# Handing out a side tile's twelve products in pieces of four between the units of windowed attention

## The chip, the cores and the metric

The kernel runs on one core of a Trainium2 chip. The metric is the device time of one execution, in microseconds (us); the median of several runs is compared. One execution of each kernel is also taken with the hardware profiler, and everything said about where time goes comes from that execution's trace. The engines are called as the profile calls them: PE does the matrix products (PEld is its weight load), ACT the activations, DVE and POOL element-wise work, and SP issues the DMAs.

## The reference

Four transformer layers without a feed-forward part, alternately of two kinds, on a sequence of S = 2048 rows of width D = 512, with 32 heads of 16. Kind A is causal attention within a sliding window of 256; kind B is full attention. Each layer adds its output to its input.

```python
def _A_ref(x, wqkv, wo):                     # B the same, without the mask
    B, S, D = x.shape
    H = 32; Dh = D // H; W = 256
    qkv = (x @ wqkv).reshape(B, S, 3, H, Dh).transpose(2, 0, 3, 1, 4)
    q, k, v = qkv[0], qkv[1], qkv[2]
    scores = jnp.einsum("bhqd,bhkd->bhqk", q, k) * (Dh ** -0.5)
    idx = jnp.arange(S)
    mask = (idx[:, None] - idx[None, :] >= 0) & (idx[:, None] - idx[None, :] < W)
    scores = jnp.where(mask[None, None], scores, -1e9)
    p = _softmax(scores, axis=-1)
    o = jnp.einsum("bhqk,bhkd->bhqd", p, v)
    return o.transpose(0, 2, 1, 3).reshape(B, S, D) @ wo

x = A_x
x = x + _A_ref(_layernorm(x), A_wqkv, A_wo)
x = x + _B_ref(_layernorm(x), B_wqkv, B_wo)
x = x + _A_ref(_layernorm(x), A_wqkv, A_wo)
x = x + _B_ref(_layernorm(x), B_wqkv, B_wo)
```

## The kernel before, in words

Layers 0 and 2 are the sliding ones, layers 1 and 3 the full ones. Within a layer the queries are taken in four chunks `c` of 512 rows, and the 32 heads in eight groups `qd` of four.

**Units of attention.** In a sliding layer, `attn_win` cuts the work of one (c, qd) into three units `u`, so a layer has 4 x 8 x 3 = 96 units. A unit has three steps. First `exps` runs twice, once for each pair of heads: PE writes scores into a PSUM tile `s` (L731), ACT turns it into probabilities `e` (L735), and POOL zeroes the two triangles of the window's edges in `e` (L802, L805). The pool of `s` has two buffers, and a unit uses both, so the first scores of the next unit wait until ACT has read the first tile, and its second scores until ACT has read the second. Then, two units late (`flush(2)`), PE multiplies the probabilities by the values (the products into `acc`, L812). Then `sd.step()` may put other work on PE.

**Side work.** That other work is everything that is not attention: the projections to keys, queries and values (`project`, `values`) for later chunks and for the next layer, and the output projection (`wo`) with the layer norm behind it. It is cut into tiles: a tile is twelve matmuls, four blocks of the inner dimension times three terms of a split into half-precision parts, accumulated in one PSUM bank and then read out. In a sliding layer the key and query tiles are read out by ACT (`sp`, L506), followed by a square on ACT (`sq`, L519) and a second half on DVE (L509); value tiles by ACT (L637); output tiles by DVE (L653). These tiles come from a pool of two banks, `b`, which they share with the sums of squares (`squares`, L546), taken in rotation. Each work is a Python generator; `mms` is the part that records the matmuls. In a full layer `mms` yields after each of its matmul steps; in a sliding layer it does not yield, so a tile is one run of twelve.

**What sets the order.** PE's instructions keep the order in which the program records them. The other engines' order in a sliding layer is made by a scheduler from readiness and priority. `Side` is the planner: it holds the works of one chunk and their cost on a model clock (0.222 us for a matmul, `MM`). At step k of n, work is due up to cost x k / (n - 2), and `step` goes on taking from the works until what is spent reaches what is due:

```python
            s0, due = self.spent, self.cost * self.k / (self.steps - 2)
            while self.q and self.spent < due and self.spent - s0 < 3:
                c = self.one()
                if c is None or c < 0 and self.spent - s0 >= 2 and due - self.spent < 4:
                    break
```

A negative cost marks the end of a tile. `one` picks the first work that is ready, unless a tile is open (`PH["busy"]`), in which case it must go on with the same work (`PH["last"]`); before, only the full layers open a tile in this sense. `finish` gives out what is left at the end of a chunk, and the parts between the layers (`all_of`) run outside any phase. `phase(l)` sets `PH["full"]` and `PH["win"]`.

Of the kernel before, what the change touches and what calls it, by code (L numbers as in the profile page):

```python
# [30 lines left out]
SCALE = DH ** -0.5  # L31
MM = 0.222
HEAD_START = 100
EB, XB, XNB, WB, VB, OB = 6, 4, 4, 2, 3, 5
RINGS = WB, VB
L_MIN = 2.0 ** -90
# [153 lines left out]
def fast_path(ctx, tc, flag, a_x, a_wqkv, a_wo, b_wqkv, b_wo, out):  # L190
# [199 lines left out]
    def mms(ps, pairs, after=1.6, us=MM):  # L390


        PH["busy"] = PH["full"]
        for i, (a, b) in enumerate(pairs):
            if PH["full"]:
                for g in range(0, P, 32):
                    for r in range(2):
                        k = slice(R * r, R * r + R)
                        nc.tensor.matmul(ps[g:g + 32, r], a[k, g:g + 32], b[k], start=(i == 0), stop=(i == len(pairs) - 1),  # L399
                                         skip_group_check=True)  # L400
            else:
                nc.tensor.matmul(ps, a, b, start=(i == 0), stop=(i == len(pairs) - 1))  # L402
            spent(us)
            if i < len(pairs) - 1:
                if PH["full"]:
                    yield us
            else:
                PH["free"] = clock[0] + (2.0 if PH["full"] else after)
                PH["busy"] = False
    TERMS = ((0, 0), (0, 1), (1, 0))  # L410

    def join(dst, ps, scale=1 / WS):
# [65 lines left out]
    def project(l, s, c, act, ht=None):  # L478


        ty, n = l % 2, f"{l}_{s}_{c}" + ("" if ht is None else f"_h{ht}")
        w = weights(ty, s, n, *((0, D, 0) if ht is None else (ht * P, (ht + 1) * P, not act)))
        yield wait(8)
        xc = XC[l, c]
        if s == 0:
            dst = rows(qs[ty, c])
        elif ty == 0:
            dst = rows(kw[c])
        else:
            dst = rows(kf)[:, :, c * QC:(c + 1) * QC]  # L490
        sqs = {}
        for t in range(NHT) if ht is None else (ht,):
            ps = bank()
            w0 = t * P if ht is None else 0
            yield from mms(ps, [(w[:, k, a, w0:w0 + P], xc[:, b, k, :]) for a, b in TERMS for k in range(NC)], 2.2)
            if not PH["full"]:
                settle(not sqs)
            with tc.high_priority(HEAD_START):
                if PH["full"]:
                    drain(1)  # L500
                    j = vp.tile([P, QC], F32, name=f"j{n}_{t}", tag="j")
                    join(j, (ps[:, 0], ps[:, 1]))
                else:
                    sp = vp.tile([P, 2, QC], F16, name=f"sp{n}_{t}", tag="sp", bufs=3)
                    if act:
                        nc.scalar.activation(sp[:, 0], ps, AF.Copy, scale=1 / WS)  # L506
                    else:
                        nc.vector.tensor_scalar(sp[:, 0], ps, 1 / WS, None, op0=ALU.mult)
                    nc.vector.scalar_tensor_tensor(sp[:, 1], ps, 1 / WS, sp[:, 0], op0=ALU.mult, op1=ALU.subtract)  # L509
            full = PH["full"]  # L510

            def parts(t=t, sp=None if full else sp, j=j if full else None):
                if full:
                    sp = vp.tile([P, 2, QC], F16, name=f"sp{n}_{t}", tag="sp", bufs=3)
                    nc.vector.tensor_copy(sp[:, 0], j)  # L515
                    nc.vector.tensor_tensor(sp[:, 1], j, sp[:, 0], ALU.subtract)
                sq = vp.tile([P, QC], BF16, name=f"sq{n}_{t}", tag="sq", bufs=NHT)
                if act:
                    nc.scalar.activation(sq, sp[:, 0], AF.Square)  # L519
                else:  # L520
                    nc.gpsimd.tensor_tensor(sq, sp[:, 0], sp[:, 0], ALU.mult)  # L521
                sqs[t] = sq

                d = dst[8 * t:8 * t + 8].rearrange("h (d b) n -> (h d) b n", b=4)
                if s:
                    nc.sync.dma_start(d[:, 0:2], sp[:, 0:1].broadcast_to([P, 2, QC]))
                    nc.sync.dma_start(d[:, 2], sp[:, 1])
                else:
                    nc.sync.dma_start(d[:, 0:2], sp)
                    nc.sync.dma_start(d[:, 2], sp[:, 0])  # L530
            soon(0, 1.2, parts)
            yield -MM if PH["full"] else -12 * MM
        return sqs

    def squares(n, sqs):
# [71 lines left out]
    def values(l, c, act, halves=(0, 1), tiles=range(4)):  # L607

        n = f"{l}_{c}_{halves[0]}_{tiles[0]}"
        HH, D0, D1 = H // 2, halves[0] * D // 2, (halves[-1] + 1) * D // 2  # L610
        w = weights(l % 2, 2, f"v{n}", D0, D1)
        yield wait(8)
        xc = XC[l, c]
        dst = {}
        if l % 2:
            for h in halves:
                m = l, h, c // 2
                if m not in V:
                    V[m] = wp.tile([P, 8, HH, DH + 1], F32, name=f"vt{l}_{h}_{c // 2}", tag="vf", bufs=NQ)
                    nc.gpsimd.memset(V[m][:, :, :, DH:], 1.0)  # L620
                dst[h] = V[m][:, 4 * (c % 2):4 * (c % 2) + 4]
        else:
            vt = V[l, c] = wp.tile([P, 4, H, DH + 1], F32, name=f"vt{n}", tag="vw", bufs=VB)
            nc.gpsimd.memset(vt[:, :, :, DH:], 1.0)
        us = MM * (D1 - D0) / D
        for i in tiles:
            ps = bank()[..., :D1 - D0]
            yield from mms(ps, [(xc[:, b, k, i * P:(i + 1) * P], w[:, k, a, :D1 - D0]) for a, b in TERMS for k in range(NC)], us=us)
            src = ps.rearrange("p r (h d) -> p r h d" if PH["full"] else "p (h d) -> p h d", d=DH)
            for x, h in enumerate(halves if l % 2 else (None,)):  # L630
# [9 lines left out]
            yield -us if PH["full"] else -12 * us  # L640

    def wo(l, c, tail):

# [3 lines left out]
        for i in range(4):  # L647
# [11 lines left out]
            yield -MM if PH["full"] else -12 * MM  # L659
        if PH["full"]:  # L660
            yield from norm(l + 1, c, xs, tail)

# [220 lines left out]
    class Side:  # L883
# [13 lines left out]
        def one(self, force=False):  # L897

            drain()
            if PH["full"] and PH["busy"]:  # L900
                return self.piece(PH["last"])
            if force:
                self.prefetch()
# [3 lines left out]
            if now:  # L907
                i = now[0]
# [332 lines left out]
```

## Time and profile before

| | |
|---|---|
| median of 3 runs | 2760.06 us (2759.93 to 2761.41) |
| the profiled execution | 2759.5 us, of which its span is 2757.7 us |
| PE busy | 2496.1 us, 91% of the span |
| ACT busy | 2362.9 us, 86% |
| DVE busy | 1094.9 us, 40% |
| POOL busy | 515.8 us, 19% |
| mean granted TensorE clock | 0.988 |

The shares are averages over stages with different limits. The units of layer 0 lie between about 53 and 435 us of the span, those of layer 2 between about 1448 and 1727 us; the full layers take most of the rest. A row of the wait view names who waited, for whom, the total, the number of waits and the longest; a row of a timeline gives the start, the length and, in brackets, the idle time before it with what ended it.

### The profile page before, as it was taken

What the parts mean: (1) busy time and instruction counts of PE and PEld (TensorE: products, weight loads), DVE (VectorE), ACT (ScalarE), POOL (GpSimd) and SP (SyncE); (2) the same over time, 40 slices, a digit from 0 to 9 for tenths busy, and PEclk for the clock granted to TensorE, in tenths of its full rate; (3) what the DMA queues carried; (4) which work ended last, traced back from release to release, by engine and by line L of the source; (5) the groups of instructions that cost most, each with busy time, mean ns of one, the idle gap of its engine ahead of it and who ended that gap; (6) DMA issues with size and microseconds to landing.
All of it is one profiled execution on the core that took longest, in us unless ns stands there. A gap on an engine that the chain in (4) does not pass through costs nothing.

```text
span 2757.7 us, 112292 instructions
## 1 busy us (share of the span) xinstructions
PE 2496.1 (91%) x50513; PEld 1100.3 (40%) x50513; DVE 1094.9 (40%) x2314; ACT 2362.9 (86%) x2683; POOL 515.8 (19%) x1074
## 2 busy tenths in 40 slices
PE   7888989999989999999998898899899999998987
PEld 3233334444433344444443333534444444433332
DVE  5564554122343335325326566323333333333333
ACT  4556654899999999999995667399999999999997
POOL 1445552001000000100105678100000000000000
PEclk9999999999999999999999999999999999999999
DMA  8888856322342224324225565623232333333332
GB/s 286 226 241 240 244 178 191 96 83 82 100 120 79 86 93 137 102 78 126 93 73 169 157 181 143 175 72 109 84 107 90 98 97 104 112 104 123 114 120 103
DMA packets 335035, 359.67 MB, mean 130 GB/s; under 512 B 113616, under 2 KB 250320, under 8 KB 328144
## 3 DMA queue, kind: packets, MB, share of 16 engines
q1 hardware_dynamic: 334544, 352.40, 42.3%
q8 instruction: 397, 6.50, 1.0%
q14 instruction: 94, 0.77, 0.1%
HBM read 239.60 MB, written 96.99 MB: 122 GB/s over the span
## 4 chain that ended last, share of the span: by engine, by line
ACT 56%; PE 23%; issue 11%; DVE 5%; DMA 3%; POOL 2%; SPq 0%; ACTq 0%; DVEq 0%; POOLq 0%
ACT e L735 55%; PE b L402 10%; PE acc L812 3%; PE acc L779 3%; PE bs L402 2%; PE s L731 2%; PE s L727 2%; PE b L399 1%; POOL e L802 1%; POOL e L805 1%; DMA qt<-qs 1%; DMA kt<-kw 0%; DMA wr<-in_A_wo_dram 0%; DVE ot L694 0%; DMA w<-wd 0%
## 5 line engine op out<-in xcount | busy, mean ns | idle before, releaser
L735 ACT ACTIVATE e<-s 128x1024 f32<-128x1024 f32 (+2 forms) x2432 | 2238.8, 1058 | 121.0 <-PE s L731 95.3
L779 PE MATMUL acc<-e,vt 64*17 64x512 f32 x16384 | 1085.0, 590 | 1.3 <-issue 1.3
L727 PE MATMUL s<-qt,kt 64*32 64x512 f16 x16384 | 849.0, 380 | 130.4 <-ACT e L735 106.6
L727 PEld LDWEIGHTS <-kt 64*32 64x32 f16 x16384 | 406.7, 89 | 944.2 <-issue 868.8
L779 PEld LDWEIGHTS acc<-e,vt 64*17 64x17 f32 x16384 | 280.5, 92 | 61.1 <-issue 1.5
L805 POOL TENSOR_SCALAR_AFFINE_SELECT e<-e 128x256 f32<-128x256 f32 x512 | 224.9, 446 | 196.5 <-ACT e L735 195.4
L802 POOL TENSOR_SCALAR_AFFINE_SELECT e<-e 128x256 f32<-128x256 f32 x448 | 198.1, 449 | 114.1 <-ACT e L735 112.3
L712 POOL TENSOR_TENSOR oh<-o,oh 128x512 f16<-128x512 f32 x31 | 36.1, 1165 | 938.1 <-DVE oh L711 884.8
L812 PE MATMUL acc<-e,vt 128*17 128x384 f32 (+2 forms) x2816 | 204.7, 396 | 5.3 <-POOL e L802 4.0
L731 PE MATMUL s<-qt,kt 64*128 64x384 f16 (+2 forms) x1408 | 129.0, 280 | 64.0 <-ACT e L735 38.2
L415 DVE TENSOR_SCALAR sa<-acc 128x512 f32<-128x512 f32 x64 | 44.3, 692 | 335.4 <-PE acc L779 335.4
L402 PE MATMUL b<-xc,w 128*128 128x512 f16 x696 | 166.1, 390 | 7.0 <-DMA w<-wd 5.8
L677 DVE SCALAR_TENSOR_TENSOR x<-b,x 128x512 f32<-128x512 f32 x122 | 83.9, 688 | 193.0 <-PE b L399 189.8
L402 PEld LDWEIGHTS <-w 128*128 128x128 f16 x816 | 77.4, 100 | 122.8 <-issue 35.8
L521 POOL TENSOR_TENSOR sq<-sp 128x512 bf16<-128x512 f16 x28 | 41.0, 1463 | 442.2 <-DVE sp L515 427.6
L506 ACT ACTIVATE sp<-b 128x512 f16<-128x512 f32 x58 | 34.7, 598 | 103.3 <-PE b L402 91.2
L731 PEld LDWEIGHTS <-kt 64*128 64x128 f16 x1408 | 54.4, 94 | 167.6 <-issue 137.0
L521 POOL TENSOR_TENSOR sq_h<-sp_h 128x512 bf16<-128x512 f16 x27 | 40.1, 1484 | 409.8 <-DVE sp_h L515 409.8
L399 PE MATMUL b<-wo,oh 64*32 64x512 f16 x2592 | 109.9, 376 | 6.2 <-DVE x L677 3.1
L399 PE MATMUL b<-xc,w 64*32 64x512 f16 x2688 | 110.9, 376 | 3.0 <-DVE j L416 2.3
L399 PE MATMUL b<-xc,w_h 64*32 64x512 f16 x2592 | 104.4, 376 | 4.1 <-DVE km L562 3.9
L415 DVE TENSOR_SCALAR j_h<-b 128x512 f32<-128x512 f32 x27 | 18.7, 691 | 218.7 <-PE b L399 187.6
(136 smaller groups left out, 1874.8 us busy)
## 6 DMA issues: line engine op xcount, KB each, us to landing
kt<-kf SPq DMA_DIRECT2D x128, 512.0 KB
qt<-qs SPq DMA_DIRECT2D x128, 256.0 KB
xd<-x SPq DMA_DIRECT2D x96, 256.0 KB
x<-xd SPq DMA_DIRECT2D x96, 256.0 KB
w<-wd SPq DMA_DIRECT2D x22, 1024.0 KB
kt<-kw SPq DMA_DIRECT2D x64, 256.0 KB
qs<-sp SPq DMA_DIRECT2D x48, 256.0 KB
wo<-wd SPq DMA_DIRECT2D x12, 1024.0 KB
```

Of the source, the lines that this page charges most:

```text
L399: nc.tensor.matmul(ps[g:g + 32, r], a[k, g:g + 32], b[k], start=(i == 0), stop=(i == len(pairs) - 1), skip_group_check=True)
L402: nc.tensor.matmul(ps, a, b, start=(i == 0), stop=(i == len(pairs) - 1))
L415: nc.vector.tensor_scalar(dst, ps[0], scale, None, op0=ALU.mult)
L521: nc.gpsimd.tensor_tensor(sq, sp[:, 0], sp[:, 0], ALU.mult)
L677: nc.vector.scalar_tensor_tensor(xs[i], p, 1 / WS, xs[i], op0=ALU.mult, op1=ALU.add)
L727: nc.tensor.matmul(ps[g:g + 32, h], kt[R * h:R * h + R, pr, kc + g:kc + g + 32], qt[R * h:R * h + R, pr], start=True, stop=True, skip_grou ...
L731: nc.tensor.matmul(ps[:, h, s0:s0 + wd_], kt[R * h:R * h + R, pr, kc:kc + P], qt[R * h:R * h + R, pr, qc:qc + wd_], start=True, stop=True)
L735: nc.scalar.activation(e[:, :, w0:w1], ps[:, :, w0:w1], AF.Exp, scale=SCALE)
L779: nc.tensor.matmul(acc[r][32 * h:32 * h + DH + 1, :], V[l, qd // 4, j // 8][k, j % 8, 4 * (qd % 4) + h, :], es_[h // 2][k, h % 2, :], star ...
L802: nc.gpsimd.affine_select(v, v, pattern=[[0, 2], [-1, P]], compare_op=ALU.is_gt, fill=0.0, base=0, channel_multiplier=1)
L805: nc.gpsimd.affine_select(v, v, pattern=[[0, 2], [1, P]], compare_op=ALU.is_ge, fill=0.0, base=0, channel_multiplier=-1)
L812: nc.tensor.matmul(a[32 * h:32 * h + DH + 1, q * P:(q + nb) * P], V[l, (4 * c + j) // 4][:, j % 4, 4 * qd + h, :], es_[h // 2][:, h % 2, s ...
```

## The change

In a sliding layer a tile may now stop after four and after eight of its twelve matmuls. `mms` marks the tile as open in sliding layers too, and yields after each piece of four the cost of four. `last` gives the cost of a tile's last piece, 4 x 0.222 us in a sliding layer where it was 12 x 0.222. An open tile is carried on before any other work is picked. Full layers and the parts between the layers keep their steps.

```diff
+PIECE = 4
...
     def mms(ps, pairs, after=1.6, us=MM):
-        PH["busy"] = PH["full"]
+        PH["busy"] = PH["full"] or PH["win"]
         for i, (a, b) in enumerate(pairs):
...
             spent(us)
             if i < len(pairs) - 1:
                 if PH["full"]:
                     yield us
+                elif PH["win"] and i % PIECE == PIECE - 1:
+                    yield PIECE * us
             else:
                 PH["free"] = clock[0] + (2.0 if PH["full"] else after)
                 PH["busy"] = False
+    def last(us):
+        return -(1 if PH["full"] else PIECE if PH["win"] else 12) * us
...
-            yield -MM if PH["full"] else -12 * MM          # project; wo the same, values with us
+            yield last(MM)
...
         def one(self, force=False):
             drain()
-            if PH["full"] and PH["busy"]:
+            if PH["busy"]:
                 return self.piece(PH["last"])
```

**PE, layer 2, the second chunk, between two units.** `s_1_2_0` and `s_1_2_1` are scores of neighbouring units, `acc` the product with the values of an earlier unit, `b` an output tile's bank. Before:

```order
L731 MATMUL s_1_2_0_1_29868<-qt_1_2_29739,kt_1_2_29738 128x384
L812 MATMUL acc_82<-e_1_1_1_0_29776,vt_0_0_0_15544 17x256 x2
L812 MATMUL acc_82<-e_1_1_1_1_29785,vt_0_0_0_15544 17x256 x2
L812 MATMUL acc_82<-e_1_1_1_0_29776,vt_1_0_0_21586 17x256 x2
L812 MATMUL acc_82<-e_1_1_1_1_29785,vt_1_0_0_21586 17x256 x2
L731 LDWEIGHTS kt_1_2_29738
L731 MATMUL s_1_2_1_0_29886<-qt_1_2_29739,kt_1_2_29738 128x256
```

And now, in the changed kernel:

```order
L819 MATMUL acc_82<-e_1_1_1_1_29774,vt_1_0_0_21586 17x256 x2
L403 LDWEIGHTS oh_0_5_29428
L403 MATMUL b_29806<-wo_0_29669,oh_0_5_29428 128x512
L403 LDWEIGHTS oh_0_7_29666
L403 MATMUL b_29806<-wo_0_29669,oh_0_7_29666 128x512
L403 LDWEIGHTS oh_0_7_29666
L403 MATMUL b_29806<-wo_0_29669,oh_0_7_29666 128x512
L403 LDWEIGHTS oh_0_7_29666
L403 MATMUL b_29806<-wo_0_29669,oh_0_7_29666 128x512
L738 LDWEIGHTS kt_1_2_29723
L738 MATMUL s_1_2_1_0_29886<-qt_1_2_29724,kt_1_2_29723 128x256
```

Where the products with the values were followed at once by the next unit's scores, four of an output tile's twelve matmuls now stand between them.

**ACT, layer 2, around the end of a query tile.** `e_1_0_0` to `e_1_0_2` are the three units of one head group, `sp_0_3_0` and `sq_0_3_0` the reading out and the square of a query tile. Before:

```order
L735 ACTIVATE e_1_0_0_1_29612<-s_1_0_0_1_29607 128x1024
L506 ACTIVATE sp_0_3_0_29634<-b_29621 128x512
L735 ACTIVATE e_1_0_1_0_29646<-s_1_0_1_0_29641 128x1024
L519 ACTIVATE sq_0_3_0_29637<-sp_0_3_0_29634 128x512
L735 ACTIVATE e_1_0_1_1_29655<-s_1_0_1_1_29650 128x1024
```

And now:

```order
L742 ACTIVATE e_1_0_0_1_29612<-s_1_0_0_1_29607 128x1024
L742 ACTIVATE e_1_0_1_0_29635<-s_1_0_1_0_29630 128x1024
L742 ACTIVATE e_1_0_1_1_29644<-s_1_0_1_1_29639 128x1024
L513 ACTIVATE sp_0_3_0_29683<-b_29621 128x512
L742 ACTIVATE e_1_0_2_0_29695<-s_1_0_2_0_29690 128x1024
L526 ACTIVATE sq_0_3_0_29686<-sp_0_3_0_29683 128x512
L742 ACTIVATE e_1_0_2_1_29705<-s_1_0_2_1_29700 128x1024
```

The reading out has moved one unit later, and stands as before ahead of the next unit's first exponential, with the square behind that exponential.

**PE, layer 0, the second chunk, where sums of squares stand between two query tiles.** `b_1805` and `b_1882` are two neighbouring tiles, and `b_1867` the sums of squares; the pool `b` has two banks. Now:

```order
L403 LDWEIGHTS w_0_2_1489
L403 MATMUL b_1805<-xc_2_957,w_0_2_1489 128x512
L553 LDWEIGHTS hsum
L553 MATMUL b_1867<-sq_1_2_0_1519,hsum 32x512
L553 LDWEIGHTS hsum
L553 MATMUL b_1867<-sq_1_2_1_1612,hsum 32x512
L553 LDWEIGHTS hsum
L553 MATMUL b_1867<-sq_1_2_2_1712,hsum 32x512
L553 LDWEIGHTS hsum
L553 MATMUL b_1867<-sq_1_2_3_1769,hsum 32x512
L403 LDWEIGHTS w_0_2_1489
L403 MATMUL b_1882<-xc_2_957,w_0_2_1489 128x512
```

Before, the sums of squares were followed by a unit's scores and products, and the next tile came behind those:

```order
L546 MATMUL b_1820<-sq_1_2_3_1772,hsum 32x512
L731 LDWEIGHTS kt_1_2_1636
L731 MATMUL s_1_2_0_0_1838<-qt_1_2_1637,kt_1_2_1636 128x128
L731 LDWEIGHTS kt_1_2_1636
L731 MATMUL s_1_2_0_0_1838<-qt_1_2_1637,kt_1_2_1636 128x128
```

Two banks on, a tile gets the bank of the tile before the sums; now nothing but the sums of squares stands between the end of that tile and the first matmul that needs its bank.

More of the change, by code (lines that the diff above doesn't have):

```diff
@@ L639, in values @@
                     nc.vector.tensor_scalar(to, fr, 1 / WS, None, op0=ALU.mult)
-            yield -us if PH["full"] else -12 * us
+            yield last(us)
     def wo(l, c, tail):
@@ L658, in wo @@
                 yield from norm(l + 1, c, xs, tail)
-            yield -MM if PH["full"] else -12 * MM
+            yield last(MM)
         if PH["full"]:
```

## The prediction

> **What bounds the kernel now.** I read the table of busy time by stage first, here the first two chunks of layer 0, the bulk of the first full layer and the four chunks of layer 2.
>
> ```profile
> core 0: us, PE busy (x) PEld busy (x) DVE busy (x) ACT busy (x) POOL busy (x), PEclk, DMA share, GB/s
> 53.00:137.00 84.00, 69.60 (x516) 24.40 (x517) 39.83 (x98) 48.03 (x72) 35.77 (x91) 0.88 0.86 241
> 137.00:240.00 103.00, 84.18 (x718) 32.92 (x715) 63.59 (x151) 60.02 (x80) 49.89 (x122) 0.92 0.87 241
> 450.00:1440.00 990.00, 925.22 (x22679) 419.44 (x22678) 338.86 (x682) 953.38 (x1049) 59.46 (x46) 1.00 0.33 101
> 1448.00:1523.00 75.00, 64.51 (x512) 23.74 (x512) 43.37 (x104) 42.59 (x63) 38.90 (x92) 0.95 0.58 175
> 1523.00:1596.00 73.00, 63.96 (x687) 26.02 (x680) 44.59 (x107) 50.69 (x58) 54.51 (x134) 1.00 0.59 172
> 1596.00:1667.00 71.00, 64.29 (x688) 26.44 (x687) 41.28 (x97) 48.63 (x56) 50.33 (x125) 1.00 0.55 160
> 1667.00:1727.00 60.00, 54.10 (x631) 20.55 (x625) 43.08 (x96) 46.38 (x49) 51.51 (x125) 1.00 0.51 137
> ```
>
> The full layer belongs to ACT (953 of 990 us), and the instruction order of both full layers is the same on PE in the two kernels, so I put no change there. In the sliding layers PE is the busiest engine in every row, but it idles: 9.0 us of 73 in the second chunk of layer 2, for instance. The change moves no work off PE; it can only win that idle time. So the next view is PE's waits, in layer 0 (first fence) and layer 2.
>
> ```profile
> PE s L731 <- ACT e L735: 14.8, 22, 1.6
> PE s L731 <- DMA kt<-kw: 13.5, 2, 7.4
> PE b L402 <- DMA w<-wd: 5.8, 1, 5.8
> PE s L731 <- DMA qt<-qs: 4.3, 1, 4.3
> PE acc L812 <- POOL e L802: 3.5, 2, 2.8
> PE b L402 <- DVE km L562: 1.2, 1, 1.2
> ```
>
> ```profile
> PE s L731 <- ACT e L735: 23.5, 43, 1.1
> PE s L731 <- DMA qt<-qs: 4.6, 2, 3.8
> PE acc L812 <- POOL e L802: 0.5, 1, 0.5
> ```
>
> In both layers the scores wait for the exponentials that must clear their PSUM buffer: 14.8 + 23.5 = 38.3 us, many short waits. Layer 0 has few, long waits for loads besides. How the short waits arise is seen in the timeline of PE, at the start of the second chunk of layer 2.
>
> ```profile
> 1527.93 0.61 PE L731 MATMUL s<-qt,kt 64*128 64x256 f16 x8
> 1528.47 1.06 PE L812 MATMUL acc<-e,vt 128*17 128x384 f32 x16
> 1529.60 0.39 PE L731 MATMUL s<-qt,kt 64*128 64x384 f16 x4
> 1531.03 0.39 PE L731 MATMUL s<-qt,kt 64*128 64x384 f16 x4 [1.04 <-ACT e L735]
> 1531.35 1.06 PE L812 MATMUL acc<-e,vt 128*17 128x128 f32 x16
> 1532.35 2.76 PE L402 MATMUL b<-xc,w 128*128 128x512 f16 x12
> 1535.04 0.61 PE L731 MATMUL s<-qt,kt 64*128 64x128 f16 x8
> ...
> 1542.15 0.61 PE L731 MATMUL s<-qt,kt 64*128 64x384 f16 x8
> 1542.69 1.06 PE L812 MATMUL acc<-e,vt 128*17 128x128 f32 x16
> 1543.72 0.39 PE L731 MATMUL s<-qt,kt 64*128 64x128 f16 x4
> 1544.64 0.39 PE L731 MATMUL s<-qt,kt 64*128 64x128 f16 x4 [0.52 <-ACT e L735]
> ```
>
> The unit at 1527.93 has no side tile: after 1.67 us PE is at the next unit's scores, and its second four must wait 1.04 us. At 1542.15 the same, with 0.52 us. A unit with a tile of twelve (2.76 us) is long enough for ACT to catch up, and then ACT has nothing to do. So PE alternates between units that are too short for ACT and units that are longer than ACT needs. ACT's own rows show what makes the first wait the longer one: a query tile's reading out and its square stand in ACT's queue between the exponentials.
>
> ```profile
> 1528.04 0.60 ACT L506 ACTIVATE sp<-b 128x512 f16<-128x512 f32 x1 [1.90 <-PE b L402]
> 1528.53 1.02 ACT L735 ACTIVATE e<-s 128x1024 f32<-128x1024 f32 x1
> 1529.43 0.63 ACT L519 ACTIVATE sq<-sp 128x512 bf16<-128x512 f16 x1
> 1529.95 1.94 ACT L735 ACTIVATE e<-s 128x1024 f32<-128x1024 f32 x2
> ```
>
> **The change, part by part.** *What it evens out.* Counted in PE's order, 93 of the 192 sliding units have no side matmul before (31 in layer 0, 62 in layer 2), and 48 after (19 and 29). The matmuls per chunk are the same. In the second and third chunk of layer 2, most units now carry four.
>
> *What four matmuls are worth.* Twelve take 2.76 us with the last one's 0.38 us in it (its length in the row of matmul groups below), so one step is (2.76 - 0.38) / 11 = 0.216 us and a piece 0.86 us.
>
> ```profile
> L402 PE MATMUL b<-wo,oh 128*128 128x512 f16 x192 | 44.2, 380 | 0.0
> ```
>
> Second scores may start 1544.64 - 1542.15 = 2.49 us after the preceding unit's first scores where ACT has exponentials alone, and 1531.03 - 1527.93 = 3.10 us after them where a query tile is read out in between. PE on its own arrives at 1.67 + 0.33 = 2.00 us without a side matmul, so it waits about 0.5 and 1.1 us, as the rows show. With one piece it arrives at 2.86 us: no wait in the first case, 0.24 us in the second. With two pieces it arrives at 3.72 us: none in either. So one piece is enough to close the common gap.
>
> *A, waits that go.* I take the waits in proportion to units without side work. Layer 0: 14.8 / 31 = 0.48 us each, times 12 fewer, 5.7 us. Layer 2: 23.5 / 62 = 0.38 us each, times 33 fewer, 12.5 us. Together -18.2 us. What hides the pieces is ACT's time for the exponentials; where a unit gets no piece (the ends of chunks, where the works have run out), the wait stays.
>
> *B, does POOL come up behind it?* After the change POOL's window edges are the next thing: 54.51 + 50.33 us in chunks two and three of layer 2, against 63.96 + 64.29 us on PE. PE stays later by 23 us there. In the last chunk POOL has 51.51 us against 54.10, but A takes only 6 units' worth (2.3 us) of the 60 there. No charge.
>
> *C, reading out in short units.* Layer 2 reads out 14 key and query tiles on ACT inside its units:
>
> ```profile
> L506 ACT ACTIVATE sp<-b 128x512 f16<-128x512 f32 x12 | 7.2, 598 | 25.2 <-PE b L402 19.9 <-DMA xd<-x 3.0 <-POOL e L802 1.3
> L506 ACT ACTIVATE sp_h<-b 128x512 f16<-128x512 f32 x2 | 1.2, 598 | 4.5 <-PE b L402 4.5
> ```
>
> Each can cost 0.24 us if a unit of one piece follows: 0 to 3.4 us, I take +2. In layer 0 most units carry eight or twelve.
>
> *D, more switches on PE.* Groups of side matmuls between products with the values and scores go from 99 to 144. What one more switch costs shows in three rows from layer 0, where every unit has twelve:
>
> ```profile
> 310.87 0.61 PE L731 MATMUL s<-qt,kt 64*128 64x256 f16 x8
> ...
> 312.40 2.76 PE L402 MATMUL b<-wv,xc 128*128 128x512 f16 x12
> 315.10 0.61 PE L731 MATMUL s<-qt,kt 64*128 64x384 f16 x8
> ```
>
> Such a unit lasts 4.23 us; an empty one 1.67 us plus 12 x 0.216 = 2.59 us makes 4.26. The switch costs -0.03 us, nothing. The other end is a first weight load wholly exposed at each switch, 98 ns by this row:
>
> ```profile
> L402 PEld LDWEIGHTS <-oh 128*128 128x128 f16 x192 | 17.5, 98 | 25.0 <-issue 5.7 <-DMA qt<-qs 0.4
> ```
>
> 45 x (-0.03 to 0.10) is -1.4 to +4.4 us. I take +1, near the unit's row. The Trainium skill ("TensorE: Matmul & The Clock Gate", Part 3, The mechanism and what overlaps) speaks against the change here: a weight load overlaps a running matmul only where the two use different row groups. By that rule, since the side weights cover all rows, D would be the upper end and the sum 3.4 us higher. The 4.23 us unit shows no such exposure, so the row decides.
>
> *E, loads in layer 0.* The loads of keys arrive when the DMA queues deliver (DMA share 0.86 and 0.87 in the first two chunks), and PE waited 13.5 us for two of them, at the fifth head group of each of these chunks. In the order PE has done 8 and 4 fewer side matmuls by those points, and must do them afterwards: 12 x 0.216 = 2.6 us, if the landings don't move. Part of A's 5.7 us lies ahead of these landings and would be swallowed as well. Bounds: 0 (SP now issues the first of these loads ahead of a query tile's stores, so it may land earlier) to 8.3 us. I take +3.
>
> *F, a bank wanted too early.* A key or query tile's reading out is ACT's 0.60 us and then this row of DVE, 0.69 us:
>
> ```profile
> L509 DVE SCALAR_TENSOR_TENSOR sp<-b,sp 128x512 f16<-128x512 f32 x12 | 8.2, 686 | 22.0 <-ACT sp L506 22.0
> ```
>
> At two places in layer 0 a tile's first matmul now follows so closely on the end of the tile that last held its bank that the reading out is exposed. The nearest row is PE's wait of 1.2 us for a reading out (km, above); below it lies nothing, above it 0.60 + 0.69 = 1.3 us. I take 2 x 1.2 = +2.3.
>
> Sum: -18.2 + 2 + 1 + 3 + 2.3 = -9.9 us. The profiled execution took 2759.5 us (span 2757.7), 0.6 under the median of 2760.06, so the median becomes 2750.
>
> **The rivals.** *Nothing is lost on the way.* C, D and F are nothing and the loads of layer 0 come as early as PE does: -18.2 us, 2742. For it: the 4.23 us unit without any loss, and the issue of loads moved ahead. Against: the high DMA share in chunks one and two.
>
> *Layer 0 gives nothing.* The loads set the pace there, so its 5.7 us are lost and E's 2.6 and F's 2.3 are paid, while layer 2 gives 12.5 - 2 - 1 = 9.5: -4.6 us, 2755, within the 0.2% (5.5 us) that a measurement of this kernel can tell from no change. For it: two waits of up to 7.4 us for loads.
>
> *ACT falls behind the readings out, and the result is slower.* In A and C I let one piece absorb nearly all of a reading out. If instead each key or query tile that now ends in a unit of one or two pieces costs the 1.04 us of the row at 1531.03, because ACT holds `sp` and `sq` in its queue ahead of the exponentials and never gets the long unit in which it caught up, then 15 such tile ends beyond those in the sum take back its 9.9 us and 5.5 more. There are 14 in layer 2 and about 40 in layer 0; with 25 of them the time is 2750 + 26 - 2 = 2774, and it is slower by over 0.2% from about 16 on. Against it: ACT's load, 50.69 us of 73. A further stall for a load like the 7.4 us ones, twice over, would end near the same place.
>
> That the change does nothing is excluded: the order shows the pieces.
>
> **How the numbers follow.** Forecast 2750: 0.42. Nothing lost, 2742: 0.26. Layer 0 gives nothing, 2755: 0.17. Slower: 0.15. The first two are faster by over 0.2%, so 0.68 faster, 0.17 the same, 0.15 slower. The range goes from 2738 (full gain, switches at -1.4 us, and some 3 us of load waits gone with earlier issues) to 2764 (all charges at their upper ends, 3.4 + 4.4 + 8.3 + 2.6 = 18.7 us, which cancel A, and half of one further 7.4 us stall), which leaves out most of the slower rival.
>
> **What would show it right or wrong.** In the changed profile the scores' wait for ACT should fall from 23.5 to about 11 + 2 us in layer 2 and from 14.8 to about 9 in layer 0; the second chunk of layer 2 should shrink from 73 to 66 or 67 us, with PE's busy time there unchanged. D is wrong if PE's busy time in the sliding stretches grows by more than 2 us; E, if the waits for `kt` differ from 13.5 us by more than 3; F, if no wait of side matmuls for ACT's `sp` or DVE's `x` appears. The prediction fails as a whole if units with one piece still show waits of 0.5 us or more for ACT, or if POOL's wait in layer 2 rises above 5 us.

## The result and the profile after

Over five runs the changed kernel takes 2746.32 us in the median (2744.14 to 2750.35), against 2760.06 us for the kernel before (2757.69 to 2761.41, five runs on the same chip). The ratio is 0.9951, with a 95% interval of 0.9939 to 0.9964: 13.7 us less, where 9.9 were forecast, and inside the predicted range. The profiled execution has a span of 2744.6 us, 13.1 under the span before.

Where these 13.1 us lie is seen by cutting both spans at the same points of the program (first scores and last scores of a layer, from PE's rows). Each row is one profiled execution. The rows below the first two are the changed kernel once more, and the variants of the next section:

| kernel | layer 0 | layer 1 | layer 2 | between 2 and 3 | layer 3 | median |
|---|---|---|---|---|---|---|
| before | 381.8 | 951.0 | 277.1 | 57.9 | 953.6 | 2760.1 |
| after | 371.6 | 952.9 | 265.8 | 64.8 | 953.4 | 2746.3 |
| again | 372.2 | 953.7 | 265.7 | 66.8 | 953.3 | 2746.5 |
| l0only | 368.7 | 953.9 | 275.7 | 57.6 | 957.5 | 2754.3 |
| l2only | 383.0 | 950.9 | 262.3 | 66.8 | 954.4 | 2756.2 |
| lastwhole | 371.1 | 955.7 | 267.7 | 58.0 | 957.3 | 2746.3 |
| lastearly | 372.3 | 953.6 | 268.1 | 55.9 | 953.6 | 2739.3 |
| piece6 | 381.4 | 954.7 | 266.5 | 60.2 | 956.4 | 2754.6 |
| piece2 | 372.3 | 951.0 | 262.4 | 65.9 | 956.7 | 2745.8 |
| nobehind | 368.6 | 954.7 | 260.9 | 66.4 | 953.2 | 2743.0 |
| early68 | 372.0 | 953.8 | 269.9 | 56.2 | 953.4 | 2739.8 |
| woact | 364.3 | 950.4 | 261.3 | 67.3 | 953.8 | 2745.0 |
| best | 370.5 | 953.1 | 268.4 | 55.2 | 953.7 | 2738.7 |
| best2 | 371.6 | 953.7 | 270.8 | 54.4 | 954.1 | 2744.9 |

Layer 0 gained 10.2 us, layer 2 gained 11.3, the stretch behind layer 2 lost 6.9, and layer 1, whose order is the same, took 2.0 more. The four chunks of layer 2 in the changed kernel, in the columns of the table that the prediction began with:

```profile
core 0: us, PE busy (x) PEld busy (x) DVE busy (x) ACT busy (x) POOL busy (x), PEclk, DMA share, GB/s
1439.00:1511.00 72.00, 64.64 (x527) 22.80 (x516) 43.96 (x106) 43.78 (x64) 38.63 (x93) 0.98 0.62 190
1511.00:1583.00 72.00, 64.40 (x680) 24.79 (x679) 45.22 (x105) 52.01 (x58) 55.44 (x134) 0.97 0.57 160
1583.00:1651.00 68.00, 65.70 (x688) 25.37 (x690) 42.84 (x98) 49.57 (x55) 51.96 (x125) 0.95 0.61 177
1651.00:1708.00 57.00, 51.73 (x625) 19.97 (x624) 37.39 (x85) 45.81 (x49) 50.11 (x125) 1.00 0.44 127
```

They went from 75, 73, 71 and 60 us to 72, 72, 68 and 57. PE's busy time is about what it was, 246.5 us in place of 246.9 over the four. What PE waits for now, in layer 0 and then in layer 2 (total, number, longest, in us):

```profile
PE s L738 <- ACT e L742: 8.6, 14, 2.0
PE s L738 <- DMA kt<-kw: 7.1, 2, 6.4
PE b L403 <- DVE km L569: 5.5, 1, 5.5
PE acc L819 <- POOL e L809: 4.6, 2, 4.1
```

```profile
PE s L738 <- ACT e L742: 11.9, 22, 1.1
PE s L738 <- DMA kt<-kw: 4.7, 1, 4.7
PE b L403 <- issue: 4.4, 1, 4.4
PE s L738 <- DMA qt<-qs: 3.6, 2, 2.3
PE acc L819 <- POOL e L809: 0.8, 2, 0.4
```

The waits for the exponentials are down from 14.8 to 8.6 us and from 23.5 to 11.9. Four single waits are new or longer: 5.5 us for DVE's `km` in layer 0 (1.2 before), 4.1 us for POOL there (2.8 before), 4.7 us for keys in layer 2, and 4.4 us that is put down to "issue". The last is behind layer 2. How the short waits went is plain from PE's timeline in the second chunk of layer 2, where before a unit without side work and a unit of twelve took turns:

```profile
1525.82 0.61 PE L738 MATMUL s<-qt,kt 64*128 64x384 f16 x8
1526.36 1.06 PE L819 MATMUL acc<-e,vt 128*17 128x128 f32 x16
1527.35 1.04 PE L403 MATMUL b<-wo,oh 128*128 128x512 f16 x4
1528.32 0.61 PE L738 MATMUL s<-qt,kt 64*128 64x128 f16 x8
1528.86 1.06 PE L819 MATMUL acc<-e,vt 128*17 128x256 f32 x16
1529.85 1.04 PE L403 MATMUL b<-wo,oh 128*128 128x512 f16 x4
```

A unit with one piece lasts 1528.32 - 1525.82 = 2.50 us, its eight scores are one unbroken group, and no row has a bracket.

Counted over every unit of layer 2 in the trace: before, all of the 23.5 us stand behind the 62 units without side matmuls (0.38 us each); after, 10.5 of the 11.9 us stand behind the 29 such units (0.36 each), and 1.4 us behind the 40 units with one piece (0.04 each). Units with two or three pieces led to none.

### The profile page after: what moved, and what is told of

Read it like the earlier page. It is cut to its first block, busy times and chain, and to the rows that moved or that the text cites. A ratio compares the mean times of both kernels' runs of the same rounds, so it can differ in the third digit from the quotient of the medians.

```text
span 2744.6 us, 112286 instructions
## 1 busy us (share of the span) xinstructions
PE 2497.0 (91%) x50513; PEld 1091.8 (40%) x50513; DVE 1095.0 (40%) x2314; ACT 2371.2 (86%) x2683; POOL 518.2 (19%) x1074
## 4 chain that ended last, share of the span: by engine, by line
ACT 55%; PE 24%; issue 11%; DVE 6%; DMA 3%; POOL 1%; SPq 0%; ACTq 0%; DVEq 0%; POOLq 0%
ACT e L742 54%; PE b L403 10%; PE acc L819 5%; PE s L738 3%; PE acc L786 2%; PE bs L403 2%; PE s L734 2%; PE b L400 1%; DMA kt<-kw 1%; DVE ot L701 1%; DMA x<-in_A_x_dram 0%; DMA w<-wd 0%; DVE xh L449 0%; DVE xh L455 0%; DVE sa L423 0%
## 5 line engine op out<-in xcount | busy, mean ns | idle before, releaser
L403 PE MATMUL b<-xc,w 128*128 128x512 f16 x696 | 171.6, 394 | 10.3 <-DVE km L569 5.5
L738 PE MATMUL s<-qt,kt 64*128 64x384 f16 (+2 forms) x1408 | 122.8, 281 | 40.8 <-ACT e L742 20.5
L422 DVE TENSOR_SCALAR vt<-b 128x256 f32<-128x256 f32 (+1 forms) x36 | 18.3, 509 | 213.3 <-PE b L400 194.9
```

Source lines behind the costliest of these rows:

```text
L422: nc.vector.tensor_scalar(dst, ps[0], scale, None, op0=ALU.mult)
L738: nc.tensor.matmul(ps[:, h, s0:s0 + wd_], kt[R * h:R * h + R, pr, kc:kc + P], qt[R * h:R * h + R, pr, qc:qc + wd_], start=True, stop=True)
```

## The experiments

All times are compared with runs of the kernel before on the same chip. The edits act on the sliding layers' order, or on a queue. `PH["piece"]` stands in place of `PIECE`, set per chunk.

**One layer at a time.** Pieces in layer 0 alone:

```diff
             for c in range(NQ):
+                PH["piece"] = 12 if l == 2 else 4
```

> Pieces of four in layer 0 only, runs of twelve in layer 2. Theory (each layer's gain is its own idle time won back, and the two add): layer 0 gives the 10 us that its stretch shrank by in the changed kernel, so about 2750 us, and the stretch between layers 2 and 3 is back at 58 us. Rival (the gain of layer 0 was a lucky landing of two loads, not the pieces): the waits for kt move again and the time is anywhere between 2750 and 2760.

Measured: 2754.26 us (2749.2 to 2756.62), ratio 0.9979 [0.997, 0.9988]. Layer 0 took 368.7 us, 13.1 under before, and the stretch behind layer 2 stayed at 57.6. So the layer-0 part gains by itself, and PE's waits for keys there are 6.3 us, much as in after. By its time alone the rival is not excluded: 2754.3 us is not the theory's 2750 and lies in the rival's span. The total gained only 5.7 us; in this profile, whose own time is 2751.68 us, layers 1 and 3 took 2.9 and 4.0 us more than before's.

Pieces in layer 2 alone (`12 if l == 0 else 4`):

> Pieces of four in layer 2 only. Theory: layer 2 shrinks by 11 us and the stretch behind it grows by 7 us as in the changed kernel, so about 2756 us; PE's wait for ACT in layer 2 is 12 us against 23.5 before. Rival (the longer stretch behind layer 2 comes from something that layer 0 shifted): 58 us behind layer 2, and 2749 us.

Measured: 2756.24 us (2752.31 to 2759.49), 0.9985 [0.9976, 0.9994]. Layer 2 is 14.8 us shorter and the stretch behind it 8.9 longer, PE's waits for ACT in layer 2 are 11.3 us, and the total is the theory's: pieces in layer 2 bring their own loss with them. The layers that each variant leaves as they were serve as repeats: layer 0 with runs of twelve took 381.8 and 383.0 us, layer 2 with runs of twelve 277.1 and 275.7. The two parts' gains, 5.7 and 3.7 us, add up to 9.5 where both together give 13.7; the intervals are 2.5 us to either side for each, and the pace of the full layers (below) is in them.

**The stretch behind layer 2.** The 6.9 us sit at one place. PE's timeline there, after and then before; the row with twelve matmuls is the last key tile for layer 3, which PE takes up when the units of layer 2 have run out:

```profile
1707.61 0.83 PE L819 MATMUL acc<-e,vt 128*17 128x384 f32 x4 [0.38 <-POOL e L809]
1712.81 4.25 PE L403 MATMUL b<-xc,w_h 128*128 128x512 f16 x12 [4.37 <-issue]
```

```profile
1726.94 0.83 PE L812 MATMUL acc<-e,vt 128*17 128x384 f32 x4 [0.51 <-POOL e L802]
1727.70 2.76 PE L402 MATMUL b<-xc,w_h 128*128 128x512 f16 x12
```

The tile's input `xc` comes from DMA transposes, these from a layer norm, and that from the last output tile. The wait is put down to "issue", but in the trace PE's sequencer stands until 1712.75 us at a wait for two semaphores, and one of them is set by the last of these transposes, which lands at 1712.72. SP's timeline has both ends of the chain, the store of that tile's result (`xd<-x`) and the last transpose, after and then before:

```profile
1694.33 0.34 SPq L661 DMA_DIRECT2D xd<-x  x1
...
1709.27 1.24 SPq L477 DMA_TRANSPOSE xc<-xh  x1
```

```profile
1706.55 0.34 SPq L654 DMA_DIRECT2D xd<-x  x1
...
1722.23 1.23 SPq L470 DMA_TRANSPOSE xc<-xh  x1
```

The chain is as long as before (14.9 us from store to last transpose, 15.7 before). But PE reaches the key tile 1727.70 - 1706.55 = 21.2 us behind the store before, and 1708.44 - 1694.33 = 14.1 us behind it after. Spreading the side work over all units lets its last output tile end nearer to the last unit. PE's 4.37 us of idling is then followed by twelve matmuls at 4.25 us in place of 2.76: together 5.9 of the 6.9 us.

If that is the cause, runs of twelve in the last chunk alone undo it, and so does an earlier due time for that chunk's work. First `PH["piece"] = 12 if (l, c) == (2, 3) else 4`:

> Pieces of four everywhere but in the last chunk of layer 2, which has runs of twelve. Theory (spreading that chunk's output tiles ends the last of them later, so that its layer norm and transposing DMAs are late for the last key tile): the 4.4 us wait of that tile and the half clock behind it go, the stretch behind layer 2 is back at 58 to 59 us, and since the last chunk had almost the same waits for ACT before and after, the time is about 2741 us. Rival (the stretch grew because PE arrives earlier while SP and the DMA queues do not): the wait stays and the time stays at 2746 us.

Measured: 2746.34 us (2744.12 to 2747.43), 0.9952 [0.9938, 0.9965]. The stretch is 58.0 us and its wait is gone, as the theory said; the total is no lower than after's, which is the rival's number. Layer 2 took back 1.9 us, and layers 1 and 3 were 2.7 and 3.9 us longer in this profile. The theory's total missed. Then pieces everywhere, with the last chunk due 8 units before its end in place of 2:

```diff
-            s0, due = self.spent, self.cost * self.k / (self.steps - 2)
+            s0, due = self.spent, self.cost * self.k / (self.steps - self.spare)
...
+                if (l, c) == (2, 3):
+                    sd.spare = 8
```

> Pieces of four everywhere, but in the last chunk of layer 2 the work is due over 16 steps instead of 22, so that the last output tile ends two units earlier than before the change instead of two units later. Theory: the wait of the last key tile goes while the pieces stay: 2740 us. Rival (PE arrives too early whatever the tile's end): 2746 us. If the key tile that now comes earlier waits in the middle of the chunk instead, 2744 us.

Measured: 2739.28 us (2736.51 to 2741.76), 0.9926 [0.9912, 0.9939]. The stretch is 55.9 us. Here the two columns have to be added: the last key tile's 2.76 us now stand between units of layer 2 (at 1701.79 us, with scores behind it at 1704.49) and no longer in the stretch. Layer 2 and the stretch together are 324.0 us, and 325.7 in lastwhole, against 330.6 after, 332.5 in its second profile, 329.1 and 328.6 in l2only and woact, which have the same pieces in layer 2, and 335.0 before. Two edits that act on nothing but the end of the side work remove the loss, so this cause is shown.

**The size of a piece.** Pieces of six and of two everywhere:

> Pieces of six products in place of four, everywhere else as after: 20 units of layer 0 and 38 of layer 2 stay without side work (19 and 29 after, 31 and 62 before). Theory (the gain goes with the units without side work, 0.38 us each in layer 2): PE waits for the exponentials in layer 2 come to 38 x 0.38 = 14 us (11.9 after, 23.5 before), the sliding stretch of layer 2 to about 268 us (265.8 after), the total to about 2748. Rival (the gain comes from shorter groups, whatever the empty units do): the waits stay at 12 us or rise to about 18, half way between runs of four and of twelve, and the total stays within 1 us of 2746 or rises to 2753.

Measured: 2754.63 us (2748.54 to 2757.98), 0.998 [0.9971, 0.9989]. PE's waits in layer 0 (first) and layer 2:

```profile
PE s L738 <- DMA kt<-kw: 16.3, 3, 10.3
PE s L738 <- ACT e L742: 6.9, 14, 1.0
```

```profile
PE s L738 <- ACT e L742: 15.1, 28, 1.1
```

In layer 2 the theory's rule holds: 15.1 us for 14 forecast, and 14.9 of them stand behind the 38 units without side work, so the number of such units decides and not the length of a group. In layer 0 the waits for ACT fall too, to 6.9 us, and the whole gain is lost to the loads of keys, 16.3 us. The total missed for that reason and for longer full layers.

> Pieces of two: 18 units of layer 0 and 23 of layer 2 without side work, but units with two products alone. Theory (a unit has to hold about 0.5 us of side work for the exponentials not to be waited for; two products are 0.43 us): the common wait of 0.5 us falls to 0.1 us in a unit of one piece, so layer 2 loses another 2 us of waits (to about 10) and the total is about 2744 to 2747, the stretch behind layer 2 staying near 65 us, since the side chain ends as late. Rival (every switch between side products and attention costs PE up to 0.1 us): some 60 more switches cost up to 6 us, PE's busy time in layer 2 grows by as much, and the total is 2750 to 2752.

Measured: 2745.81 us (2745.16 to 2749.81), 0.9955 [0.9941, 0.9968], the same as pieces of four. PE's waits for ACT in layer 2 fell to 7.5 us, where about 10 were expected. Its 262.4 us for layer 2 are no shorter than kernels with pieces of four show: 265.8, 265.7, 262.3 and 261.3 us in after, again, l2only and woact. Taking all of layer 2, PE's time outside idling is 245.6 us with 33 groups of side matmuls (before), 244.3 with 66 (after) and 245.2 with 72 (pieces of two). So this run has only 6 more switches there than after, not the 60 of the expectation, and tests the rival little. It is the step from before to after that does: 33 more switches at 0.1 us would have added 3.3 us, and the time fell by 1.3. The rival, up to 0.1 us a switch, falls.

**The bank behind the sums of squares.** After's longest new wait in layer 0, in PE's timeline and then in DVE's:

```profile
159.79 0.40 PE L553 MATMUL b<-sq,hsum 128*32 128x512 bf16 x4
165.74 3.57 PE L403 MATMUL b<-xc,w 128*128 128x512 f16 x8 [5.55 <-DVE km L569]
```

```profile
164.39 0.69 DVE L455 TENSOR_TENSOR xh<-xn,xh 128x512 f16<-128x512 f32 x1
165.00 0.68 DVE L569 TENSOR_REDUCE km<-b 128x1 f32<-128x512 f32 x1
165.60 0.68 DVE L516 SCALAR_TENSOR_TENSOR sp<-b,sp 128x512 f16<-128x512 f32 x1
```

PE was there at 160.2; the reading of the sums (`km`) stands in DVE's queue behind the next chunk's layer norm (`xh`), which ends at 165.1. So the tile took the bank of the sums themselves, not that of the tile before them, as the order was read ahead of the prediction: it starts at 165.74, when `km` has ended, while DVE reads the tile before the sums (`sp`) until 166.28. The variant starts no side tile in the unit of the sums:

```diff
+        PH["sums"] = True          # in squares(); cleared at each step
...
-                if c is None or c < 0 and ...
+                if c is None or PH["sums"] or c < 0 and ...
```

> Pieces of four as after, but no side tile is started in the unit in which the sums of squares of the tile before were multiplied. Theory (the bank was wanted before DVE, busy with the layer norm, had read the sums out of it): the wait of 5.5 us for km in the second chunk of layer 0 falls by the rest of one unit, 1.6 us or more, the waits of side products for DVE in layer 0 go from 9.4 us to 7 or less, and the total falls by 1 to 3 us, to 2744 or 2745. Rival (the wait is hidden by the loads of keys behind it, which arrive when they arrive): the 1.6 us come back as a longer wait for kt, and the total stays at 2746.

Measured: 2742.99 us (2741.46 to 2746.94), 0.9948 [0.9934, 0.9962]. The wait fell to 4.5 us only, by 1.0. Counted from the layer's first scores, PE now comes 1.5 us later to the tile, but DVE frees the bank 0.4 us later as well. The side products' waits for DVE in layer 0 went from 9.4 to 8.4 us, where 7 or less was expected, and the waits for keys grew from 7.1 to 10.4, the way that the rival had it. Layer 0 was 368.6 us; but the unchanged layer 0 took from 368.7 to 372.3 us in six profiles (after, again, l0only, lastwhole, lastearly, early68), so the gain there can't be told from their spread, nor the total from after's. Inconclusive.

**Earlier due times in three chunks of layer 2** (`sd.spare = (2, 6, 6, 8)[c]`), to take away the wait for keys at the third chunk too:

> Pieces of four as after, but in layer 2 the side work of chunks 1, 2 and 3 is due 6, 6 and 8 units before the chunk's end (2 after). Theory (what the spreading cost lay in chains that end late: the load of keys at the start of chunk 3 of layer 2, 4.7 us, and 6.9 us at the last key tile behind layer 2): both go, the stretch behind layer 2 is 56 to 58 us (64.8 after), layer 2 is about 262 us (265.8), less 2 us for five more units without side work, and the total is 2737 to 2740. Rival (only the last chunk matters, and ending earlier opens the waits for exponentials again): the wait for kt moves to another unit of the same length, layer 2 is 268 us and the total 2741 to 2743, no better than ending the last chunk alone early.

Measured: 2739.76 us (2738.79 to 2743.7), 0.993 [0.9917, 0.9944]. The stretch behind is 56.2 us, but the wait for keys came back as two of 2.6 us. Layer 2 grew by 4.1 us to 269.9, of which 2.76 are the last key tile, which has moved into it here too; with the stretch it makes 326.1, against lastearly's 324.0. As the rival had it, it is no better than hurrying the last chunk alone; the total is the theory's. In after, that wait comes behind SP's queue. PE's row, then SP's, where the load that ends the wait, the one issued at 1573.73 us, stands between two others and ahead of a block of 6.28 us:

```profile
1583.68 1.03 PE L738 MATMUL s<-qt,kt 64*128 64x128 f16 x8 [4.67 <-DMA kt<-kw]
```

```profile
1572.01 1.67 SPq L769 DMA_DIRECT2D kt<-kw  x1
1573.73 1.17 SPq L771 DMA_DIRECT2D kt<-kw  x1
1574.95 0.93 SPq L769 DMA_DIRECT2D kt<-kw  x1
1575.98 6.28 SPq L595 DMA_DIRECT2D qs<-m_None  x4
```

Which of these transfers held the keys back was not separated.

**The queue that the keys of layer 0 stand in.** In the first chunk of layer 0 the load of keys that PE waits for is issued behind eight loads of output weights. SP's rows of after:

```profile
87.19 7.58 SPq L322 DMA_DIRECT2D wr<-in_A_wo_dram  x8
...
96.05 0.39 SPq L769 DMA_DIRECT2D kt<-kw  x1
```

The next variant issues these eight, and the like in the second chunk (at 183.85 us in after; the expectation calls it the third), from ACT (`nc.scalar.dma_start` for `nc.sync.dma_start`):

> As after, but the eight loads of the raw output-projection weights, which hold SP's queue for 7.6 us in the first chunk of layer 0 and 6.5 us in the third, are issued from ACT's queue. Theory (keys come late because their load is queued on SP behind these eight): the load of keys awaited in the first chunk is issued up to 7 us earlier, the wait of 6.4 us there falls to 0 to 2 us, the sliding stretch of layer 0 from 371.6 to about 367 us, and the total to about 2742. Rival (the transfers themselves are the limit, the DMA engines being 0.8 busy): the keys land no earlier, or the weights take their bandwidth, and the wait stays within 1.5 us of 6.4; the total stays at 2746 or rises by ACT's issuing (8 x 0.4 us, twice).

Measured: 2744.99 us (2740.15 to 2747.92), 0.995 [0.9937, 0.9964], as after. PE waits for keys no more in layer 0, as the theory said. But it waits for ACT:

```profile
183.11 1.02 ACT L742 ACTIVATE e<-s 128x1024 f32<-128x1024 f32 x1
183.96 14.03 ACTq L322 DMA_DIRECT2D wr<-in_B_wo_dram  x6
198.11 1.94 ACT L742 ACTIVATE e<-s 128x1024 f32<-128x1024 f32 x2 [13.99 <-issue]
```

```profile
PE s L738 <- ACT e L742: 19.9, 18, 10.7
```

Six issues held ACT for 14.0 us and cost PE 10.7 in one wait; another, of 8.2 us, is for queries (`qt`). Layer 0 is 7.4 us shorter than after's all the same, and the span begins its units 10.3 us later (63.9 us against 53.6), since the first eight loads now go out at 25 to 46 us beside those of the start. The order of the start moved too, so the run shows that the keys' wait depends on what is queued and in flight around them, not on which of the two.

**The same kernel again.**

> The changed kernel once more, unaltered, beside the two others of this set: a measure of how far one and the same kernel moves from one profiled execution to the next. Theory (layers 1 and 3, whose instructions are the same in all kernels, vary by some us from one execution to the next): the sliding stretches repeat within 1 us (371.6 and 265.8 us, 64.8 behind layer 2), while layer 1 and layer 3 may lie anywhere from 950 to 957 us; the median is 2745 to 2748. Rival (each kernel has a pace of its own in layers 1 and 3): both repeat within 0.5 us of 952.9 and 953.4.

Measured: 2746.47 us (2742.3 to 2748.67), 0.9951 [0.9937, 0.9964]. Layers 0 and 2 repeat within 0.7 us and the stretch behind within 2.0, somewhat more than expected. Layers 1 and 3 repeat within 0.8 and 0.1 us: the rival was nearer. Two executions of one kernel are few, though, and something speaks against the rival: up to the end of layer 1, l0only, lastwhole, lastearly and early68 have after's order on PE, and took 953.9, 955.7, 953.6 and 953.8 us for that layer, against 952.9 and 953.7 in after's two profiles. Whether the longer full layers of l0only, lastwhole and piece6 belong to the kernel or to the one execution stays open.

**Both amendments together**, nobehind and lastearly:

> Pieces of four, with both amendments: no side tile started in the unit of the sums of squares, and the side work of the last chunk of layer 2 due 8 units before its end in place of 2. Theory (the two are independent: 3.0 us in the stretch of layer 0, about 9 us behind layer 2): layer 0 is 368 to 369 us, the stretch behind layer 2 about 56 us, the total 2734 to 2738. Rival (the gains of the first are the noise of one profile): layer 0 is 371 to 372 us and the total 2739 to 2741, that of the second amendment alone.

Measured: 2738.73 us (2734.44 to 2744.76), 0.9929 [0.9915, 0.9943]. The fastest median, 19.7 us under before on the same chip, but its interval overlaps lastearly's. Layer 0 at 370.5 us lies between the two expectations; and the three kernels with the first amendment (nobehind, best, best2) took 368.6 to 371.6 us for layer 0, where the six without it took 368.7 to 372.3. What that amendment adds is not shown. The waits of this kernel from layer 2 to the start of layer 3:

```profile
PE s L739 <- ACT e L743: 10.5, 19, 1.1
PE s L739 <- DMA kt<-kw: 4.8, 1, 4.8
PE bs L403 <- DMA w_h<-wd: 4.1, 1, 4.1
```

The 4.4 us put down to "issue" are gone; the 4.1 us at the next tile stood in before too, as 3.8 us.

**With pieces of two in layer 2 besides** (`2 if l == 2 else 4`):

> As best (both amendments), with pieces of two in layer 2 in place of four; layer 0 keeps pieces of four. Theory (two products cover nearly all of the 0.5 us that a unit waits for ACT, and more units get some, 23 without side work in place of 29 when the last chunk is not hurried): layer 2 falls from best's 268.4 us to about 265, the stretch behind it stays at 55 to 56 us, and the total is 2735 to 2737. Rival (the last chunk, due 8 units early, has its pieces given out two or three to a unit anyway, and what remains are waits for loads): layer 2 stays within 1 us of 268.4 and the total within 2 us of best's 2738.7.

Measured: 2744.92 us (2743.34 to 2747.38), 0.9944 [0.993, 0.9957]. Both missed: layer 2 grew to 270.8 us. Its waits for ACT fell from 10.5 to 8.4 us, with 26 units without side work in place of 29, but the last key tile waits 2.4 us again and a wait of 3.9 us for `xc` came up. The total was measured on another chip than best's, and the intervals of the two ratios overlap; layer 2 and the stretch together differ by 1.6 us, less than the 3.9 us by which the four profiles with after's pieces in layer 2 differ (328.6 to 332.5). So pieces of two are not shown to be better than four here, nor worse.

## Why the prediction was right, and where it was not

The total was right to 3.7 us, and as near to the rival "nothing is lost on the way" (2742, 4.3 us off). By its parts it is a mixture, and the closeness of the sum is in part luck:

*A, the waits for ACT.* Right: 18.2 us forecast; 14.8 - 8.6 and 23.5 - 11.9 make 17.8 measured. Units without side work kept 0.36 us each, and pieces of six fell near the same line (14.9 us behind 38 units, 0.39 each).

*B, POOL.* Right in layer 2: PE waits 0.8 us for it there. In layer 0, at which B did not look, the wait grew from 3.5 to 4.6 us.

*C, reading out in short units.* Right: +2 forecast; the 40 units of one piece cost 1.4 us in all. They are part of the 11.9 us, so that in layer 2 the units without side work gave 23.5 - 10.5 = 13.0 us, where A has 12.5.

*D, the switches.* +1 forecast, nothing found, at twice the number of groups. The rule quoted from the Trainium skill ("TensorE: Matmul & The Clock Gate", Part 3, The mechanism and what overlaps), which would have made it the upper end, shows no effect: a piece's row begins where the products with the values end, and the unit lasts 2.50 us, 1.67 for an empty one and 0.83 for the piece.

*E, the loads of layer 0.* Wrong in sign. I forecast waits for `kt` longer by 3 us; they fell from 13.5 to 7.1. The profiles agree on it: 13.4 us in l2only, which has before's layer 0, and 6.3 to 8.7 us in the five others with after's. The step that failed is "if the landings don't move". PE had indeed done 8 and 4 fewer side matmuls at the two places. The first wait stayed (6.1 and 6.4 us), but at the second, where PE waits 7.4 us before, the changed kernel comes at 187.9 us and finds the keys there; it waits 0.8 us for those of the next head group. SP issues the load in question 6.3 us earlier, before and after:

```profile
188.63 0.55 SPq L764 DMA_DIRECT2D kt<-kw  x1
189.23 7.52 SPq L321 DMA_DIRECT2D wr<-in_B_wo_dram  x8
```

```profile
182.33 0.49 SPq L771 DMA_DIRECT2D kt<-kw  x1
```

The loads are issued from the same stream of SP that the side tiles feed, and so they move with the order. In pieces of six the term turned the other way, 16.3 us. A change of order in layer 0 may move it by 6 us down or 3 up, and I had no means of telling which from the order alone.

*F, the bank wanted too early.* Mis-sized: 1.2 us at each of two places was forecast; one place showed 5.5 us, the other none, and the 1.2 us that stood in before are in these 5.5, so the term cost 4.3 us in place of 2.3. The step that failed is the bound of 1.3 us: I priced the reading-out by its own length, and did not ask what else is queued on DVE at that moment. The view of before's waits in layer 0 has a row that the prediction leaves out, and it is above that bound:

```profile
PE b L546 <- DVE sp L509: 3.9, 1, 3.9
```

There, at 82.31 us, the reading-out of a tile stood in DVE's queue behind the rows of a layer norm, as `km` does after the change. With this row as the nearest, two places would have been priced at 7.8 us.

*What no term had.* The stretch behind layer 2, +6.9 us, and the wait for keys in its third chunk, +4.7 us. I had looked for units that get a piece, and not at the end of the works: who waits for the last of them. The check that the second chunk of layer 2 should shrink to 66 or 67 us failed for this: it lasts 72.7, of which 4.67 is that wait; PE arrives at the next chunk's scores after 68.1.

So two errors of opposite sign stand in the total: layer 0 gave 10.2 us where terms A, E and F left 0.4, and layer 2 with the stretch behind it gave 4.4 where 9.5 were forecast. By PE's waits, layer 0's gain is 6.2 us less for ACT, 6.4 for keys, 2.0 for weights (`w`, 5.8 to 3.8) and 0.5 for queries, against 4.3 more for `km` and 1.1 for POOL. The rival "layer 0 gives nothing" is refuted by l0only, the slower rival by the cost of a unit with one piece. "Nothing is lost" was near in C and D, and wrong in F and in the stretch behind layer 2.

## What to carry to other kernels

Where an engine alternates between units that are too short for its partner and units that are too long, count the units without filler: waiting per such unit, times their number, sized the waits that went to within a microsecond (18.2 us for 17.8), though not the gain in time, which the loads and the end of the filler moved by up to 10 us a layer. Then look at what spreading does to the end of the filler: whoever consumes its last result now gets it later and comes for it earlier. Give the last stretch its work ahead of time, and price a moved reading-out by the queue of the engine that does it, not by its own length.

## What the runs showed that was not expected

PE's clock falls behind a few microseconds of idling. These rows of after cover the key tile that began behind 4.37 us of idling and the stretch that followed, then the eight matmuls behind 5.55 us in layer 0; the column behind POOL's is the granted clock:

```profile
1712.80:1717.00 4.20, 4.19 (x15) 1.45 (x15) 0.61 (x2) 0.00 (x0) 0.00 (x0) 0.63 0.00 0
1717.00:1721.00 4.00, 4.00 (x53) 2.77 (x53) 2.58 (x8) 1.61 (x3) 0.00 (x0) 1.00 0.74 180
165.70:169.20 3.50, 3.46 (x8) 0.99 (x7) 0.64 (x2) 0.00 (x0) 0.00 (x0) 0.50 1.02 403
```

The granted clock is 0.63 and 0.50, and 1.00 right after the first: a wait of 4 to 6 us costs PE a further 1.5 us or so (4.25 against 2.76 us for twelve matmuls). Within these twelve, the first seven steps take 0.38 to 0.43 us each and the last three 0.21 or 0.22. Shorter idling was free in one case: behind 2.44 us of it, in best2 (at 1705.46 us), twelve matmuls took 2.75 us; behind 3.79 us, in before (at 1765.56 us), they took 4.45.

The full layers, whose order on PE is the same in these kernels, took from 950.4 to 955.7 us (layer 1) and from 953.2 to 957.5 us (layer 3), in one profile each. The one kernel profiled twice repeated within a microsecond, but executions of one kernel can lie further apart than that: those of piece6 took from 2748.54 to 2757.98 us. What makes the difference is not known. At nearly 9 us over both layers together (1904.2 to 1913.0) it is as large as what most of these edits move, and it is why the stretches, rather than the totals, were compared here. These have a spread of their own where the order on PE is the same: 3.6 us in layer 0 (368.7 to 372.3) and 4.5 us in layer 2 (261.3 to 265.8), against gains of 10 us and more.
